# Delta-rule attention with a mixture of experts: the attention in float32 on small tiles of the array

## The chip, the cores and the metric

One core of one Trainium2 chip. The time is microseconds on the device for one execution of the whole program, the median of the runs. TensorE is PE in the profile (its weight loads PEld), VectorE is DVE, ScalarE ACT, GpSimd POOL, SyncE SP.

## The reference

Four batches, 8 heads, 768 tokens, head dimension 48 (D). Each head carries a D x D state through the tokens; the output of the heads, 384 wide, goes to a mixture of 8 experts in which a token may keep the expert of the token before it.

```python
k_n = k / (np.linalg.norm(k, axis=-1, keepdims=True) + 1e-06)
for t in range(S):
    y[:, :, t] = np.einsum('bhd,bhde->bhe', q[:, :, t], state)
    v_old = np.einsum('bhde,bhd->bhe', state, kt)
    state = state + bt[:, :, :, None] * np.einsum('bhd,bhe->bhde', kt, vt - v_old)
...
logits = np.einsum('bsd,de->bse', x, w_gate)
local_gate = 1.0 / (1.0 + np.exp(-np.einsum('bsd,de->bse', x, w_local).squeeze(-1)))
# the expert e: a fresh argmax where local_gate < 0.5 and at s == 0, else the one before
h = np.maximum(x[b, s] @ w1[e], 0.0)
out[b, s] = p[e] * (h @ w2[e])          # w1 384 x 1024, w2 1024 x 384, p the softmax of the logits
```

## The kernel before, in words

The tokens go in 24 steps of 32. In a step the 128 partitions hold 4 batches x 32 tokens, and the 8 heads lie along the free axis. Four steps make a macro step, whose preparation is shared. Every matmul operand of the attention is split into an f16 hi part and an f16 lo part, and a product is three f16 matmuls (hi hi, hi lo, lo hi).

- `K`, `norm`, `K2`, `K3` load the keys of a macro step, square and sum them (ACT, DVE), scale them by their norms, split them (`k16`), copy them apart into `KJ` (keys of two batches at columns 0 and 64), transpose `KJ` to `KT` by a DMA, and form the Gram matrices of the keys (L201).
- `T_` inverts the triangular matrices (I + beta G) of a macro step: DVE transposes (L224), a forward substitution of 15 dependent pairs of instructions on the two 16 x 16 diagonal blocks (L231, L232, nearly all on POOL), and transposes back.
- `Q` loads q and v (`qv`), splits q, spreads it to `QT`, and multiplies with the keys (L266; masked at L277).
- `Tc` adds the lower left block of the inverse by two rounds of matmuls (L292, L306), and spreads the blocks to the block-diagonal `bd`.
- `online` is the recurrence, for each half of the heads: keys times state (L329), queries times state (L336), R = v - K S (L341), U (L350), its hi and lo (L352, L353), the state in PSUM (L362, two 64-row tiles of the array), the state's hi and lo (L366, L367), the output (L372), its hi and lo (L375, L376). Every second step writes y to `xs` in DRAM, transposes it by a DMA and takes the logits (L385).

The mixture is the class `Moe`. `graph` routes the tokens of the first 20 steps, then of the last four, computes expert 0 in two lots and the expert of place 1, and loads the weights for them, all as entries of the same list as the attention. `rest` runs the other six experts (places 2 to 7) in plain program order: `upm` (L502) and `downm` (L509) on PE, `uphi` (L503) on ACT, `upt` (L504) on DVE, gathers (L490) and scatters (L492) by indirect DMAs of POOL. `overflow` is a loop that runs no iteration for tokens that fit.

The instructions of the attention and of `graph` are added to a list and issued in the order of `ORDER`, a list of numbers in the file, in which a letter names the engine where several can do the work. Buffers come from pools (`Pool_`) and are placed when their first instruction is issued. Each engine takes its own instructions in that order.

Of the kernel before, what the change touches and what calls it, by code (L numbers as in the profile page):

```python
"""Delta-rule attention followed by a top-1 mixture of experts with carried routing."""
# [13 lines left out]
class Buf:  # L15
    """a buffer of a pool, placed when its first instruction is issued"""
    def __init__(s,pool): s.pool=pool; s.slot=None; s.left=0
# [3 lines left out]
class Pool_:  # L21
    def __init__(s,tiles,name=''): s.name=name; s.tiles=tiles; s.init=[[] for _ in tiles]; s.busy=[False]*len(tiles); s.age=[-1]*len(tiles)
    def __call__(s): return Buf(s)

class Op:
    def __init__(s,fn,bufs): s.fn=fn; s.bufs=bufs; s.done=False

class Sched:
    """the instructions in program order, with what each reads, writes, writes a part of, and holds; issued in the order of ORDER.
    A function with a parameter gets the engine that ORDER names."""  # L30
    def __init__(s): s.ops=[]
    def add(s,fn,r=(),w=(),p=(),claim=()):
        bufs=list({id(x):x for x in [*r,*w,*p,*claim] if isinstance(x,Buf)}.values())
        for b in bufs: b.left+=1
        s.ops.append(Op(fn,bufs)); return s.ops[-1]
    def issue(s,order,engines):
        assert len(order)==len(s.ops)
        for n,k in enumerate(order):
            o=s.ops[int(k.rstrip("SAVPG"))]; o.done=True
            for b in o.bufs:  # L40
                p=b.pool
                if b.slot is None:
                    b.slot=min((i for i in range(len(p.tiles)) if not p.busy[i] and all(x.done for x in p.init[i])),key=lambda i:p.age[i]); p.busy[b.slot]=True
                b.left-=1
                if b.left==0: p.busy[b.slot]=False; p.age[b.slot]=n
            if k[-1] in engines: o.fn(engines[k[-1]])
            else: o.fn()


class Attn:  # L50
    NKT=9; NKJ=9; NQC=2; NBD=2; GATE=1; NKF=4; NK16=2; NQV=3; NY=2; NCMP=3; NAM=1; NLX=2; NTT=1; NTX=1; NXC=1; NPO=2; NPK=1; NPT=3; AMG=()
    def __init__(s, ctx, tc, qv,k,beta,xs,wg,wl,lg):
        s.tc=tc; s.nc=nc=tc.nc; s.xs=xs
        s.qv_,s.k,s.beta=qv,k,beta
        s.NSTEP=k.shape[0]; s.NM=s.NSTEP//4
        s.wg,s.wl,s.lg=wg,wl,lg; s.sqrts=[]
# [26 lines left out]
        s.pt=Pool_([s.pp.tile([128,512],F32,name=f"pt{i}") for i in range(s.NPT)],"pt")  # L83
        if s.GATE:
            s.wc=T([128,3,9],F32,"wc"); s.wc16=T([128,2,3,9],F16,"wc16")
            s.xt=P(1,[128,12,128],F16,"xt")
    @staticmethod
    def blk(t,z,u,p): return t[:,p,z,u,:]
    def build(s,extra=(),post=None):
        nc=s.nc; S=s.sc=Sched(); NS,NM=s.NSTEP,s.NM; add=S.add  # L90
        E_={"V":nc.vector,"G":nc.gpsimd,"A":nc.scalar,"S":nc.sync}
        s.E_=E_
# [18 lines left out]
        for f in extra: add(f)
        def zero(pool):
            for i,t in sorted(enumerate(pool.tiles),key=lambda e:(pool is s.KJ and e[0]<len(pool.tiles)-1)):
                fl=t.rearrange({3:"p a b -> p (a b)",4:"p a b c -> p (a b c)",5:"p a b c d -> p (a b c d)"}[len(t.shape)]).bitcast(F32)
                def fa(e,fl=fl):
                    if e is nc.scalar: nc.scalar.mul(fl,s.zsrc.to_broadcast(list(fl.shape)),0.0)
                    else: e.memset(fl,0.0)
                pool.init[i].append(add(fa))
# [58 lines left out]
        def K3(i,k16,k6,ii):  # L177
# [8 lines left out]
            if c==0: M["gt"]=s.gt()  # L186
# [848 lines left out]
```

## Time and profile before

| | |
|---|---|
| runs, us | 611.4, 612.09, 616.03 (median 612.09) |
| profiled execution, first to last instruction | 614.3 us |
| mean granted TensorE clock | 0.864 |
| busy PE / DVE / ACT / POOL | 473.4 / 520.8 / 346.8 / 340.8 us |
| DMA | 88.23 MB, mean 144 GB/s |
| first and last y (L376) | 76.2 and 366.6 us |

Of the profiled execution no time is known but its span, 614.3 us; it stands 2.2 us over the median of the runs. A row of a group has its line, engine, operation, what it writes and reads, partitions x elements, count, then busy us and mean ns of one, then the idle time of the engine before them and what ended it. A row of one line has min/median/max ns, and where its first and last instruction start. A row of the timeline has start, length, engine, line and count of instructions merged into one stretch. Matmuls are pipelined and their ends are modelled: how close they follow each other is read from the stretch of a burst, not from the mean of one.

### The profile page before, as it was taken

The page shows a single profiled execution, that of the slowest core. Times are in us where ns is not written, and L with a number is a line of the kernel's source. Part 1 is how long each engine was busy: PE and PEld are TensorE (multiplying, and loading weights), DVE is VectorE, ACT ScalarE, POOL GpSimd, SP SyncE. Part 2 cuts the span into 40 slices and gives each one's busy share as a digit, 9 for nine tenths or more (in the row PEclk, how much of TensorE's full clock was granted, in tenths as well). Part 3 has the DMA queues.
Part 4 walks back from the last instruction along what each step waited for, and adds up shares of the span by engine and source line. Part 5 has one row for each costly group of instructions (what it writes and reads, how often), then busy time and mean ns, then how long its engine had stood idle before and what let it go on. Part 6 is the DMA issues. An engine that isn't in the chain of part 4 may idle for free. (4 is left out here: it accounts for less than half of the span.)

```text
span 614.3 us, 19858 instructions
## 1 busy us (share of the span) xinstructions
PE 473.4 (77%) x8023; PEld 366.8 (60%) x8023; DVE 520.8 (85%) x1163; ACT 346.8 (56%) x745; POOL 340.8 (55%) x474
## 2 busy tenths in 40 slices
PE   0131677677789668687878769799999999999993
PEld 0131676677678667686777766654656555666661
DVE  7999998999899899989989998699785868597650
ACT  7567697678778777777878743213160605154220
POOL 7837686657667675757556764378843232414201
PEclk9998587588867777869867578799999999999997
DMA  5777777589899997797775617272567465666600
GB/s 191 129 163 119 165 99 131 93 162 169 126 164 165 131 145 127 122 161 158 121 191 118 127 40 253 70 227 89 145 209 211 127 194 170 187 162 221 120 16 29
DMA packets 244703, 88.23 MB, mean 144 GB/s; under 512 B 221651, under 2 KB 236047, under 8 KB 244608
## 3 DMA queue, kind: packets, MB, share of 16 engines
q1 hardware_dynamic: 241056, 76.87, 61.0%
q0 software_dynamic: 3552, 10.06, 5.2%
q8 instruction: 64, 1.05, 0.8%
q14 instruction: 31, 0.25, 0.2%
HBM read 46.34 MB, written 10.05 MB: 92 GB/s over the span
## 5 line engine op out<-in xcount | busy, mean ns | idle before, releaser
L502 PE MATMUL pt<-bd,KT 128*128 128x384 f16 (+4 forms) x432 | 92.0, 346 | 2.6 <-DVE tx L768 1.1
L502 PEld LDWEIGHTS <-KT 128*128 128x128 f16 x576 | 57.7, 102 | 44.3 <-issue 6.4
L201 PE MATMUL pt<-QC,KT 128*128 128x64 f16 x576 | 29.1, 222 | 41.7 <-DVE QC L126 28.8
L509 PE MATMUL po<-KJ,QT 128*128 128x384 f16 (+2 forms) x336 | 55.5, 326 | 0.0
L201 PEld LDWEIGHTS <-KT 128*128 128x128 f16 x576 | 26.9, 117 | 42.5 <-issue 39.6
L503 ACT ACTIVATE QT<-pt 128x384 f16<-128x384 f32 (+2 forms) x32 | 16.7, 526 | 61.9 <-PE pt L502 42.7
L509 PE MATMUL po<-KJ,L 128*128 128x384 f16 (+2 forms) x208 | 50.7, 326 | 0.0
L503 ACT ACTIVATE L<-pt 128x256 f16<-128x256 f32 (+4 forms) x40 | 18.2, 463 | 55.8 <-PE pt L502 46.1
L509 PEld LDWEIGHTS <-QT 128*128 128x128 f16 (+2 forms) x336 | 33.9, 101 | 21.1 <-issue 0.3
L329 PEld LDWEIGHTS <-KT 128*128 128x128 f16 x552 | 35.5, 117 | 16.6 <-issue 7.9
L504 DVE TENSOR_SCALAR qv<-pt 128x384 f32<-128x384 f32 (+4 forms) x56 | 33.4, 599 | 11.2 <-ACT L L503 5.5
L336 PEld LDWEIGHTS <-QT 128*128 128x128 f16 x1104 | 41.4, 107 | 1.0 <-issue 0.8
L350 PE MATMUL po<-Rs,bd 128*128 128x48 f16 x576 | 27.4, 195 | 17.7 <-DMA bd<-cmp 7.0
L492 POOL DMA_INDIRECT out_dram<-y,so x9 | 11.2, 1245 | 50.8 <-DVE y L510 50.5
L266 PE MATMUL pt<-QC,KT 128*128 128x64 f16 x576 | 31.4, 223 | 8.2 <-DVE QC L251 3.1
L329 PE MATMUL pk<-Sh,KT 128*128 128x96 f16 x368 | 30.1, 241 | 7.9 <-DVE R L341 6.5
L341 DVE SCALAR_TENSOR_TENSOR R<-pk,qv 64x192 f32<-64x192 f32 x92 | 32.4, 352 | 3.4 <-PE pk L329 1.9
L232 POOL TENSOR_TENSOR X<-X,ft 128x30 f32<-128x30 f32 (+7 forms) x75 | 31.5, 420 | 5.9
L350 PEld LDWEIGHTS <-bd 128*128 128x128 f16 x576 | 22.2, 104 | 20.2 <-issue 12.0
L509 PE MATMUL po<-KJ,X 128*128 128x384 f16 (+2 forms) x104 | 33.9, 326 | 0.0
L362 PE MATMUL Sps<-Us,KJ 64*128 64x48 f16 x1104 | 29.2, 195 | 5.4 <-DVE Us L353 4.1
L292 PE MATMUL pt<-XC,bd 128*128 128x16 f16 x576 | 21.0, 191 | 15.7 <-DVE XC L126 6.5
(316 smaller groups left out, 1503.4 us busy)
## 6 DMA issues: line engine op xcount, KB each, us to landing
KT<-in_moe_w_dram SPq DMA_DIRECT2D x24, 512.0 KB, 4.5
qv<-in_qv_dram SPq DMA_DIRECT2D x24, 448.0 KB, 4.7
KT<-in_moe_w_dram SPq DMA_DIRECT2D x20, 384.0 KB, 3.3
xs<-y SPq DMA_DIRECT2D x12, 384.0 KB, 4.4
KJ<-in_moe_w_dram SPq DMA_DIRECT2D x12, 384.0 KB, 4.6
kf<-in_k_dram SPq DMA_DIRECT2D x10, 384.0 KB, 4.2
bd<-cmp SPq DMA_DIRECT2D x58, 64.0 KB, 3.7
KJ<-k SPq DMA_DIRECT2D x65, 48.0 KB, 3.6
```

Of the source, the lines that this page charges most:

```text
L201: nc.tensor.matmul(gv[:,u,:],KT.t[:,z,u,:],KC.t[:,y,u].rearrange("r p t -> r (p t)"),start=(x==0),stop=(x==2),skip_group_check=True)
L232: eng.tensor_tensor(x[:,:,j+1:,0:k],x[:,:,j+1:,0:k],tv,op=ALU.subtract)
L266: nc.tensor.matmul(gv[:,u,:],KT.t[:,z,u,:],QC.t[:,y,u].rearrange("r p t -> r (p t)"),start=(x==0),stop=(x==2),skip_group_check=True)
L329: for uu in range(4): nc.tensor.matmul(pkv()[:,uu],KT.t[:,z,4*g+uu,:],S_.t[:,:,uu,:],start=(y_==0 and z==0 and uu==0),stop=(y_==1),skip_gr ...
L336: for p in range(2): nc.tensor.matmul(psv()[:,1,uu,:],s.blk(QT.t,z,4*g+uu,p),S_.t[:,p,uu,:],start=(y_==0 and z==0 and uu==0 and p==0),stop ...
L341: add(lambda R=R,pkv=pkv,us=us,q=q,p=p:nc.vector.scalar_tensor_tensor(R.t[q],pkv()[q,:,p,:],-2.0**-10,vb()[q,us,:],op0=ALU.mult,op1=ALU.ad ...
L350: for uu in range(4): nc.tensor.matmul(psv()[:,0,uu,:],bdv()[:,a_,4*g+uu,:],Rs.t[:,b,uu,:],start=(i==0 and b==0 and a_==2 and uu==0),stop= ...
L362: nc.tensor.matmul(s.Sps[:,p,48*u:48*u+48],KJ.t[q,a_,u,:],Us.t[q,b,uu,:],start=(i==0 and u==0 and b==0 and a_==0),stop=False,skip_group_ch ...
L502: for k in range(3): s.nc.tensor.matmul(ps,s.wv(W[k],k)[:,a,0,128*f:128*f+128],xT[:,3*b+k,:],start=(x==0 and k==0),stop=(x==2 and k==2))
L503: def uphi(s,h,ps): s.nc.scalar.activation(h,ps,AF.Relu,scale=2.0**-6)
L504: def upt(s,t,ps): s.nc.vector.tensor_scalar(t,ps,0.0,2.0**-6,op0=ALU.max,op1=ALU.mult)
L509: s.nc.tensor.matmul(po[0:m],h(a,f)[:,c:c+m],s.wv(W[k],k)[:,b,f%2,:],start=(x==0 and f==0),stop=(x==2 and f==7))
```

## The change

The attention (the class `Attn`) and the scheduler are written anew; of `Moe`, the arithmetic and the order in `rest` stay.

- The host lays k and q side by side by column (`kq`: step, pair of batches, the 48 dimensions as rows, then head, batch pair, k or q, token) beside k and v by token (`kv`). The key transposes by DMA, `KJ`, `KT`, `QT`, `QC`, `k16` and `bd` are gone.
- Matmuls are float32 calls on tiles of the array: 64 x 32 for the products over the 48 dimensions, 32 x 32 for those over 16 or 32 tokens, 32 x 64 for the state. Each batch has a tile of its own, so a product of a head is four calls.
- Nothing is split into hi and lo but y, for the mixture. The norms are read from the diagonal of the Gram matrix, and fold into beta and v.
- `ORDER` is gone. Each entry names its engines and a cost, and a list scheduler in the kernel (`Sched.order`) sorts them when the program is built: of the entries that could start within 120 ns of the earliest one, the one with the longest way to the end goes first, on the engine where it would end first.
- Pools: one `W` of 24 tiles for the keys and queries of a step and for expert weights; `po` 1 (before 2), `pk` 2 (before 1), `pt` 3 as before. The substitution is on DVE for the first macro step and on POOL after it. A macro step is prepared while the one before it runs. The weights of expert 0 are added behind step 8.

```diff
 class Sched:
-    """the instructions in program order, with what each reads, writes, writes a part of, and holds; issued in the order of ORDER.
-    A function with a parameter gets the engine that ORDER names."""
-    def __init__(s): s.ops=[]
+    HOP=70; DMA=2000; BW=170.; LOOK=120
...
+            t0=min(c[0] for c in cand)
+            t,o,x=max((c for c in cand if c[0]<=t0+s.LOOK),key=lambda c:(c[1].pri-(c[1].c[c[2]]-min(c[1].c.values()))*0-c[0]*.0,-c[0]-c[1].c[c[2]]))
...
 class Attn:
-    NKT=9; NKJ=9; NQC=2; NBD=2; GATE=1; NKF=4; NK16=2; NQV=3; NY=2; NCMP=3; NAM=1; NLX=2; NTT=1; NTX=1; NXC=1; NPO=2; NPK=1; NPT=3; AMG=()
+    NKV=5; NAM=8; NW=24; NLX=1; NPO=1; NPK=2; NPT=3; NKF=4; NFT=3; NS_=4; GATE=1
...
+        H=[(h,h%2,h//2,slice(32*h,32*h+32),slice(64*(h%2),64*(h%2)+48)) for h in range(4)]
...
+        def K(i):
+            m,c=divmod(i,4); M=mac[m]; D=st[i]
+            KQ=D["KQ"]=s.W(); g=s.pt(); am=D["am"]=s.am()
+            for j in range(2): add(lambda j=j:nc.sync.dma_start(KQ.t[64*j:64*j+48].rearrange("r u p z t -> r (u p z t)"),s.kq_[i,j]),p=[KQ],e='S',c=196608)
...
+                for u in range(8):
+                    for h,j,p,q,d in H: MM(g.t[q,64*u:64*u+64],KQ.t[d,u,p,0,:],KQ.t[d,u,p].rearrange("r z t -> r (z t)"),start=(u==0),stop=True,skip_group_check=True,tile_position=(64*j,32*h))
+            add(f,r=[KQ],w=[g],claim=[gt,am],e='P',c=900)
+            add(lambda:nc.scalar.copy(gt.t.rearrange("p t (u c) -> p u t c",c=4)[:,:,:,c],gv()[:,:,0,:]),r=[g],p=[gt],e='A',c=ca(256))
+            add(lambda:nc.vector.tensor_tensor(am.t,gv()[:,:,1,:],s.mask.unsqueeze(1).to_broadcast([128,8,32]),op=ALU.mult),r=[g,"mask"],w=[am],c=cv(256)+50)
...
+        def Tc(i):
...
+                        o=slice(32*h,32*h+16); MM(g.t[q,16*u:16*u+16],gt.t[o,:,4*u+c],TX.t[o,:,4*u+c],start=(u==0),stop=True,skip_group_check=True,tile_position=(32*h,32*h))
+            add(f1,r=[gt,TX],w=[g],claim=[QQ],e='P',c=620)
+            add(lambda:nc.scalar.copy(QQ.t[:,:,0:16],g.t[:,0:128].rearrange("p (u c) -> p u c",u=8)),r=[g],w=[QQ],e='A',c=ca(128))
...
+                    for h,j,p,q,d in H: MM(g.t[q,128+16*u:144+16*u],QQ.t[q,u,:],TT.t[q,16:32,4*u+c],start=False,stop=True,skip_group_check=True,tile_position=(32*h,32*h))
...
+            add(lambda:nc.vector.tensor_tensor(vv(),vv(),g.t[:,128:256].rearrange("p (u t) -> p u t",u=8),op=ALU.subtract),r=[g,TT],w=[(TT,c)],c=cv(128)+50)
+            add(lambda:nc.sync.dma_start(kv.t.rearrange("p z c -> p (z c)"),s.kv_[i]),w=[kv],e='S',c=393216)
...
+        def online(i):
+            py=s.po(); yv=lambda a,b:py.t[:,48*a:48*b].rearrange("p (u e) -> p u e",e=48)
...
+                            for h,j,p,q,d in H: MM(pk.t[q,48*uu:48*uu+48],KQ.t[d,4*g+uu,p,0,:],Sb.t[d,p,uu,:],start=(uu==0),stop=True,skip_group_check=True,tile_position=(64*j,32*h))
...
+                    add(lambda R=R,pk=pk,vg=vg:nc.vector.tensor_tensor(R.t.rearrange("p u e -> p (u e)"),vg(),pk.t[:,0:192],op=ALU.subtract),r=[pk,(kv,1)],w=[R],claim=[kv],c=cv(192)+40)
...
+                        for h,j,p,q,d in H: MM(pk.t[q,192+48*uu:240+48*uu],TT.t[q,:,4*(4*g+uu)+c],Rv()[q,uu,:],start=(i==0 and uu==0),stop=True,skip_group_check=True,tile_position=(32*h,32*h))
+                add(p1,r=[(TT,c),Rk],w=[pk],claim=[TT,kv],e='P',c=360)
+                add(lambda Us=Us,pk=pk:nc.scalar.copy(Us.t.rearrange("p u e -> p (u e)"),pk.t[:,192:384]),r=[pk],w=[Us],e='A',c=ca(192))
...
+                            for h,j,p,q,d in H: MM(s.Sps[d,p,48*u:48*u+48],kv.t[q,0,48*u:48*u+48],Us.t[q,uu,:],start=(i==0 and u==0),stop=False,skip_group_check=True,tile_position=(32*h,64*j))
...
+                    add(lambda Sn=Sn,g=g:nc.scalar.copy(Sn.t[0:112].rearrange("p h u e -> p h (u e)"),s.Sps[0:112,:,192*g:192*g+192]),r=["Sps"],w=[Sn],e='A',c=ca(384))
...
+        for m in range(-1,NM):
+            if m+1<NM:
+                for i in range(4*m+4,4*m+8): K(i)
+                T_(m+1)
+            if m>=0:
+                for i in range(4*m,4*m+4):
+                    Tc(i); online(i)
+                    if i in pre: pre[i](S,s)
```

More of the change, by code (lines that the diff above doesn't have):

```diff
@@ L15, with __init__ @@
 class Buf:
-    def __init__(s,pool): s.pool=pool; s.slot=None; s.left=0
+    def __init__(s,pool): s.pool=pool; s.slot=None; s.ops=[]; s.left=0; s.no=len(pool.bufs); pool.bufs.append(s)
     @property
@@ L21, with __init__, idle, at @@
 class Pool_:
-    def __init__(s,tiles,name=''): s.name=name; s.tiles=tiles; s.init=[[] for _ in tiles]; s.busy=[False]*len(tiles); s.age=[-1]*len(tiles)
+    def __init__(s,tiles,name='',free=False): s.free=free; s.name=name; s.tiles=tiles; s.bufs=[]; s.init=[[] for _ in tiles]; s.user=[None]*len(tiles); s.next=0
     def __call__(s): return Buf(s)
+    def idle(s): return [i for i,u in enumerate(s.user) if (u is None or u.left==0) and all(q.end is not None for q in s.init[i])]
+    def at(s,i): return max([0.]+[q.end for q in s.init[i]]+[q.end for q in (s.user[i].ops if s.user[i] else ())])
@@ L33, in add @@
         bufs=list({id(x):x for x in [*r,*w,*p,*claim] if isinstance(x,Buf)}.values())
[L34 to L39, printed above, removed]
+        o=Op(fn,bufs,e,c); o.boost=pri; k=lambda x:id(x) if isinstance(x,Buf) else (id(x[0]),)+x[1:] if isinstance(x,tuple) and isinstance(x[0],Buf) else x
+        for b in bufs: b.ops.append(o); b.left+=1
@@ L40, in issue @@
             for b in o.bufs:
-                p=b.pool
                 if b.slot is None:
[L43 to L46, printed above, removed]
+                    p=b.pool
+                    b.slot=min(p.idle(),key=p.at)
+                    p.user[b.slot]=b; p.next+=1
@@ new lines, in order @@
+            for b in o.bufs: b.left-=1
+            y='G' if x=='I' else x
+            busy=60. if x=='S' else 1150. if x=='I' else o.c[x]
+            E[y]=t+busy
+            if x in 'SI':
+                dma=max(dma,t)+o.c[x]/s.BW; o.end=dma+(s.DMA if x=='S' else 2500)
+            else: o.end=t+busy+(190 if x=='P' else s.HOP)
+            out.append((o,x)); s.when.append((t,busy,x,o)); avail.remove(o)
+            for q in o.succ:
+                q.need-=1; q.ready=max(q.ready,o.end)
+                if not q.need: avail.append(q)
@@ L47, in issue @@
+        assert len(out)==len(s.ops)
+        s.end=max(o.end for o in s.ops)
+        return out
+    def issue(s,engines):
+        for o,x in s.order():
+            if o.takes: o.fn(engines[x])
             else: o.fn()
 class Attn:
-    NKT=9; NKJ=9; NQC=2; NBD=2; GATE=1; NKF=4; NK16=2; NQV=3; NY=2; NCMP=3; NAM=1; NLX=2; NTT=1; NTX=1; NXC=1; NPO=2; NPK=1; NPT=3; AMG=()
-    def __init__(s, ctx, tc, qv,k,beta,xs,wg,wl,lg):
+    NKV=5; NAM=8; NW=24; NLX=1; NPO=1; NPK=2; NPT=3; NKF=4; NFT=3; NS_=4; GATE=1
@@ L82, in __init__ @@
         s.pk=Pool_([s.pp.tile([128,512],F32,name=f"pk{i}") for i in range(s.NPK)],"pk")
[L83 to L92, printed above, removed]
+        s.pt=Pool_([s.pp.tile([128,512],F32,name=f"pt{i}") for i in range(s.NPT)],"pt",True)
@@ L111, in build @@
[L111 to L118, printed above, removed]
@@ L995 @@
     with tc.manual_schedule():
[L996 to L997 removed]
+        A=Attn(ctx,tc,kq,kv,beta,xs,wg,wl,lg,M.CAP)
+        A.build(M.consts(),{8:M.early},M.graph).issue(A.E_)
         M.rest(A)
```

705 lines of the change are left out of this document (243 added, 462 removed).

## The prediction

> **What bounds the kernel now.** I read the page's first two parts, then the table of stages, then single lines for where each stage ends.
>
> ```profile
> span 614.3 us, 19858 instructions
> PE 473.4 (77%) x8023; PEld 366.8 (60%) x8023; DVE 520.8 (85%) x1163; ACT 346.8 (56%) x745; POOL 340.8 (55%) x474
> PEclk9998587588867777869867578799999999999997
> ```
> ```profile
> 60.00:75.00 15.00, 8.44 (x216) 7.97 (x216) 14.73 (x35) 8.68 (x23) 10.70 (x10) 0.50 0.75 165
> ...
> 150.00:200.00 50.00, 40.34 (x1087) 37.88 (x1086) 46.28 (x117) 39.92 (x98) 32.53 (x57) 0.76 0.94 159
> ...
> 250.00:300.00 50.00, 39.26 (x1147) 36.88 (x1149) 45.81 (x121) 38.64 (x94) 34.49 (x65) 0.83 0.83 145
> ...
> 470.00:520.00 50.00, 50.00 (x310) 29.19 (x309) 38.56 (x71) 19.38 (x29) 15.47 (x13) 1.00 0.56 163
> ```
> ```profile
> L376 DVE SCALAR_TENSOR_TENSOR y<-po,y x48: 303/347/359, 76.2 to 366.6; 128x192 f16<-128x192 f32 x48
> ```
>
> The columns of a stage are its length, then busy time (and instructions) of PE, weight loads, DVE, ACT and POOL, the granted TensorE clock, the DMA engines' share and GB/s. In 85% busy DVE two kernels are averaged. From 150 to 300 us DVE is busy 46 of 50 us and PE 40, at a clock of 0.76 to 0.83: the attention is bound by VectorE, with PE and the DMA engines (0.83 to 0.94) close behind. From 470 us PE is busy 50 of 50 at clock 1.00: the mixture is bound by PE. L376 writes a step's y: first at 76.2 us, last at 366.6. So the time is a sum of three: **76.2 us to the first y, 23 steps of (366.6 - 76.2)/23 = 12.6 us, and 614.3 - 366.6 = 247.7 us behind the last y**. The change rewrites what makes the first two.
>
> **The third term.** The experts (`rest`, `upm`, `downm`) keep their instructions. Routing and expert 0 (`graph`) keep theirs too; the order comes from the new scheduler, and 24 tiles of pool `W` stand where 18 of `KT` and `KJ` stood. Four steps, which will be shorter, cover the routing of the first 20 steps, so some of expert 0 may slide behind the last y; against that, less DVE work is left over. I take 250 us, between 243 and 262.
>
> **What goes.** The f16 hi and lo parts of k, q, X, T, R, U and S, the block-diagonal copies (`bd`, `QT`, `KJ`), the DMA transposes of the keys, the squares and norms from a second load of k. What stays of DVE, ACT and POOL work I price by rows of the same shape:
>
> ```profile
> L341 DVE SCALAR_TENSOR_TENSOR R<-pk,qv 64x192 f32<-64x192 f32 x92 | 32.4, 352 | 3.4 <-PE pk L329 1.9
> L232 POOL TENSOR_TENSOR X<-X,ft 128x30 f32<-128x30 f32 (+7 forms) x75 | 31.5, 420 | 5.9
> L231 POOL TENSOR_TENSOR ft<-L,X 128x30 f32<-128x30 f32 (+7 forms) x75 | 29.6, 395 | 5.4
> L367 DVE SCALAR_TENSOR_TENSOR Sl<-Sps,Sh 128x384 f16<-128x384 f32 x46 | 25.0, 543 | 1.2 <-ACT Sh L366 0.8
> L366 ACT ACTIVATE Sh<-Sps 128x384 f16<-128x384 f32 x46 | 22.3, 485 | 4.8 <-PE Sps L362 4.6
> L277 DVE TENSOR_TENSOR am<-pt,mask 64x256 f32<-64x256 f32 x48 | 20.1, 420 | 0.9
> L207 ACT COPY gt<-pt 64x256 f32<-64x256 f32 x47 | 17.0, 364 | 6.1 <-PE pt L201 5.4
> L352 ACT ACTIVATE Us<-po 128x192 f16<-128x192 f32 x48 | 15.7, 328 | 20.1 <-PE po L350 19.6
> L224 DVE STREAM_TRANSPOSE L<-gt 128x256 f32<-128x256 f32 x24 | 14.7, 619 | 0.3 <-ACT gt L207 0.2
> L308 DVE SCALAR_TENSOR_TENSOR TT<-pt,mneg,TT 128x128 f32<-128x128 f32 x24 | 10.3, 428 | 0.4 <-PE pt L306 0.3
> L241 DVE STREAM_TRANSPOSE TT<-X 128x256 f32<-128x256 f32 x24 | 10.0, 426 | 0.1
> L232 DVE TENSOR_TENSOR X<-X,ft 128x30 f32<-128x30 f32 (+7 forms) x15 | 6.1, 405 | 0.5
> L231 DVE TENSOR_TENSOR ft<-L,X 128x30 f32<-128x30 f32 (+7 forms) x15 | 5.6, 376 | 0.4
> L164 DVE RECIPROCAL rr<-t 128x32 f32<-128x32 f32 x5 | 1.7, 344 | 0.0
> ```
>
> DVE in a step: am 0.42 (both halves in one now), two R at 0.35, the subtraction from TT 0.43, y's lo 0.54, v by the norms 0.55 (a 384-element pass, like y's). Once in four steps: ten transposes at 0.43 to 0.62, ten small ones at no more than 0.34, two products of 256 at some 0.5 (L277's kind): 9 us, so 2.2 a step. Sum **4.9 us**. ACT: 0.36 for gt, 0.3 for QQ (less than L352's 0.33), two U at 0.33, two S and y at 0.49: **2.8 us**. POOL: 15 x (0.395 + 0.420) us of substitution in four steps, and a clear of X: **3.3 us**. None of them carries 12.6 us any more.
>
> **The DMA engines.** By the shapes, a step brings 393 KB of kq and 393 KB of k and v, writes 197 KB of xs and transposes 197 KB: 1.18 MB. At 145 to 159 GB/s, the rate of the old attention, that is 7.4 to 8.1 us; at the 163/0.56 = 291 GB/s that the large rows of the weights would reach at full share, 4.1 us. The key loads have rows of 4 KB, so I take it nearer the lower end, 5 us, hidden behind PE. Expert 0's weights (3.1 MB) come on top in some steps.
>
> **PE, which I expect to bound.** A step has 256 calls now: 32 in `K` (64 columns moving), 32 in each half of `Tc` (16 columns), and ten groups of 16 (48 columns: KS, qS, U, the state, y, twice). Before it had 264 in f16, so the count doesn't fall. The price of a call is what no row shows.
>
> ```profile
> 200.02 0.27 PE L362 MATMUL Sps<-Us,KJ 64*128 64x48 f16 x8 [0.47 <-DVE Us L353]
> 200.23 0.47 PE L350 MATMUL po<-Rs,bd 128*128 128x48 f16 x12
> ...
> 200.95 0.50 PE L329 MATMUL pk<-Sh,KT 128*128 128x96 f16 x8
> ...
> 202.44 0.37 PE L362 MATMUL Sps<-Us,KJ 64*128 64x48 f16 x16
> ```
> ```profile
> 376.07 0.30 PEld L576 LDWEIGHTS pt<-sc,blk 128*128 128x128 f32 x2 [0.96 <-issue]
> ```
> ```profile
> 371.95 0.60 PE L385 MATMUL pt<-wc,xt 128*128 128x9 f16 x18
> ```
> ```profile
> L362 PE MATMUL Sps<-Us,KJ x1104: 178/192/221, 73.5 to 350.9; 64*128 64x48 f16 x184
> ```
> ```profile
> L329 PE MATMUL pk<-Sh,KT 128*128 128x96 f16 x368 | 30.1, 241 | 7.9 <-DVE R L341 6.5 <-DVE QT L126 1.0 <-ACT Sh L366 0.2
> ```
> ```profile
> L576 PEld LDWEIGHTS pt<-sc,blk x4: 186/238/334, 325.7 to 376.2; 128*128 128x128 f32 x4
> L576 PE MATMUL pt<-sc,blk x4: 244/317/400, 325.7 to 376.2; 128*128 128x20 f32 x2, 128*128 128x4 f32 x2
> ```
>
> Four readings. (1) Two calls of L576 stand as four loads and four matmuls: a float32 call is a pair of each. (2) Two f32 loads of 128 columns take 0.30 us where one takes 0.19, so they start 0.11 us apart: 0.85 ns a column. The f16 stream of L329 starts (0.50 - 0.24)/7 = 0.037 us apart for 96 columns: 0.39 ns a column. I take 0.82 ns a column for f32, in load and stream. (3) L362 puts two 64-row tiles side by side: 16 matmuls of 48 columns start (0.37 - 0.19)/15 = 12 ns apart, so two tiles turn over every 24 ns, where the full array of L350 needs 24 ns for one. Tiles do overlap. (4) L362's eight end at 200.29, so the last starts at 200.10, and L350 at another tile size starts 0.13 us later instead of 0.024: a change of tile size costs 0.1 us.
>
> If the four tiles of a round run at once, 48 columns cost 2 x 40 ns a round, a group of four rounds 0.32 us; `K` has eight rounds of 2 x 52 ns, 0.83 us; `Tc` twice eight rounds of 2 x 26 ns (the load of 32 columns), 0.83. Sum 0.83 + 0.83 + 3.2 = 4.9 us, and half of L385's 0.60: 5.2 at full clock. At the granted clock of the stages above, some 0.78, 6.6 us. Program order changes the tile size about 12 times a step: 1.2 us. With 0.3 us of waits, **8.1 us a step**. Bounds: 6.4 at full clock without waits; one tile at a time 21 (below). Matmuls 12 ns apart, as close as L362 ever shows, would make 512 x 12 = 6.1 in place of 4.9, so 9.6. A half's chain of a step is KS, R, U, its copy, the state, its copy: three groups at 0.32 + 0.19 us, 0.35 + 0.33 + 0.49, together 2.7 us; two halves in a row 5.4, under 8.1, so the chain is hidden while PE has other work. The new waits: `po` has one buffer, so the next step's qS waits for both passes over y, 0.49 + 0.54, beside four groups of KS and state; and what the fixed order puts behind a waiting group on PE waits with it. The 0.3 us stand for these, between nothing and the 2.7 of a half's chain laid bare.
>
> **The first term.**
>
> ```profile
> 0.81 1.84 SPq L139 DMA_DIRECT2D kf<-in_k_dram  x4
> ```
> ```profile
> 3.38 1.00 ACT L144 ACTIVATE QC<-kf 128x384 f32<-128x384 f32 x2
> ```
>
> A load issued at 0.81 us is used at 3.38; eight kq loads at 0.46 us each put four steps' keys on chip by about 8 us. Then `K` 1.2 with the last step's, gt 0.4, four transposes 2.5, norms 2.5, products 1.1, the first substitution on DVE 15 x (0.376 + 0.405) = 11.7, six transposes 3.0, `Tc` 2.2, U and y 2.5. First y at **36 us** for 76.2, between 30 and 45.
>
> **Sum.** 36 + 23 x 8.1 + 250 = 472 us beside the profiled 614.3. That execution's span stands 2.2 us over the median of the runs, 612.09, so **470 us**. The range of this case alone, steps of 7 to 10.3 us: 445 to 521.
>
> **Rivals.** Break-even is a step of (614.3 - 36 - 250)/23 = 14.3 us.
>
> *The tiles wait for each other, the slower side.* 160 calls of 80 ns, 32 of 104, 64 of 52 one after another are 19.5 us, with changes and logits 21: 36 + 483 + 250 - 2 = 767 us. For it: no row shows more than two tiles at once, nor f32 in one. Against it: L362's two do overlap. Chance 0.08.
>
> *Only the calls that write one bank from four row tiles wait* (`Tc`, U and y; KS, qS, `K` and the state pair rows with other columns or banks). Then 3.3 for `Tc`, 64 x 80 ns = 5.1 for U and y, 0.83 + 6 x 0.32 for the rest: 11.2, with changes and logits 12.7 a step: 576 us. L362's two tiles write two banks, so it neither shows nor excludes this. The Trainium skill, page "TensorEngine Tiling (Array Packing)", section Restrictions and Gotchas, states just that: different row tiles cannot access the same PSUM bank at once. No run here shows it. Chance 0.12.
>
> *The clock stays at half*, as in 60 to 75 us (0.50 with PE busy 8.4 of 15), since short bursts of a quarter of the array may not lift it: 5.2/0.5 + 1.2 = 11.6 a step, 551 us. Against it: 0.76 and more as soon as PE is busy 80%. Chance 0.13.
>
> *Each matmul has a floor of one turn-over*, 24 ns as L350's, tiles or not: 512 x 24 ns = 12.3, with changes and logits 13.8: 601 us, nearly no change. L362's 12 ns speaks against it. The Trainium skill, "TensorE: Matmul & The Clock Gate", Part 1, gives a floor of about 25 ns start to start however few columns; the trace agrees for one tile and not for two. Chance 0.04.
>
> *All goes well*: full clock, no waits, 6.4 a step, 431 us. Chance 0.14.
>
> **How the numbers follow.** Main case 0.49. 428 to 590 leaves out the waiting tiles (0.08), the floor (0.04) and a third of the best case: 0.17. Faster by over 1% (about what a measurement of this kernel tells from no change): main, best, half clock, bank and most of the floor: 0.89; within 1%: 0.02; slower: 0.09.
>
> **What would show it.** The first y's instruction near 36 us and the last near 222; DVE below 65% and PE above 85% busy in the attention; state matmuls of 16 calls (32 records) in 0.5 us with their drain; 247 to 253 us behind the last y. The prediction is wrong if PE's rounds take over 150 ns, if the clock lies under 0.6, or if the scheduler's order leaves PE waiting for DVE copies, which shows as idle PE before KS.

## The result, and the profile after

The changed kernel takes **696.21 us** (median of four runs, 691.12 to 697.3) against 612.28 for the kernel before on the same chip (611.4 to 616.03): an estimated ratio of 1.1336, 95% interval 1.1281 to 1.1391. The forecast was 470. Of all profiles below, one is of a slow run, that of `e4_bf16_once` (539.37 us, its other run 528.79). The profiled execution has a span of 694.0 us. The page of the changed kernel:

```profile
span 694.0 us, 30098 instructions
PE 534.0 (77%) x13903; PEld 406.0 (58%) x13903; DVE 300.0 (43%) x719; ACT 158.9 (23%) x308; POOL 142.8 (21%) x278
PEclk9999998565555555555555558686899999999997
q8 instruction: 109, 1.79, 1.1%
```

VectorE, which bounded the attention before, is down from 521 busy us to 300, as forecast, and PE's 8023 matmul records have become 13903 (a float32 call is two). The last row is a queue that I had read past: 109 packets and 1.79 MB, so 16 KB each. Its packets go with PE's instructions: 13903 matmuls and as many loads are 27806 = 108.6 x 256, and in the kernel before 16046 = 62.7 x 256 stand beside 64 packets.

The line that writes a step's y, which cuts the time into its three terms, and two stretches of the table of stages:

```profile
L284 DVE SCALAR_TENSOR_TENSOR y<-po,y x24: 524/554/569, 67.7 to 400.1; 128x384 f16<-128x384 f32 x24
```
```profile
100.00:150.00 50.00, 41.47 (x1718) 36.04 (x1714) 16.33 (x41) 12.82 (x29) 13.10 (x31) 0.74 0.31 87
150.00:200.00 50.00, 39.52 (x1710) 35.19 (x1705) 16.15 (x43) 11.10 (x27) 13.65 (x32) 0.50 0.24 60
```

| | first y | a step | behind the last y |
|---|---|---|---|
| before | 76.2 | 12.6 | 247.7 |
| forecast | 36 | 8.1 | 250 |
| after | 67.7 | (400.1 - 67.7)/23 = 14.45 | 694.0 - 400.1 = 293.9 |

All three terms missed: 31.7 us, 23 x 6.35 = 146 us and 43.9 us make the 222 between 472 and 694. In the two stretches shown no engine but PE is busy even 17 of 50 us, the DMA engines are at 0.24 to 0.31, and PE is busy only 40 of 50. So what holds a step? The waits of PE between 100 and 350 us, with the sum in us, the number of them and the longest:

```profile
PE pt L236 <- issue: 13.9, 10, 5.1
PE pt L231 <- issue: 10.3, 9, 2.5
PE po L260 <- issue: 7.4, 6, 2.0
PE po L281 <- issue: 6.5, 5, 4.3
PE Sps L273 <- issue: 5.4, 5, 3.1
PE pk L254 <- issue: 3.6, 6, 1.2
PE pt L236 <- DVE nT L206: 3.3, 1, 3.3
PE pt L185 <- issue: 2.5, 3, 1.7
...
PE pk L266 <- issue: 0.9, 3, 0.5
```

"issue" is a wait for nothing that the profile shows. It is 50.5 of the 250 us, 2.9 us a step; waits for another engine are small. The order in time on PE shows where it falls:

```profile
203.75 0.54 PE L260 MATMUL po<-S,W 48*32 48x48 f32 x14
206.27 0.55 PE L260 MATMUL po<-S,W 48*32 48x48 f32 x17 [1.98 <-issue]
206.61 0.29 PE L254 MATMUL pk<-S,W 48*32 48x48 f32 x3
206.63 0.28 PE L260 MATMUL po<-S,W 48*32 48x48 f32 x1
206.69 0.86 PE L254 MATMUL pk<-S,W 48*32 48x48 f32 x29
207.47 1.50 PE L281 MATMUL po<-Us,am 32*32 32x48 f32 x64
208.91 0.56 PE L273 MATMUL Sps<-Us,kv 32*48 32x48 f32 x14
210.28 0.64 PE L273 MATMUL Sps<-Us,kv 32*48 32x48 f32 x18 [0.81 <-issue]
```

PE stops in the middle of a group, 14 records in, where no buffer can be missing. Between the stops lie 17 + 3 + 1 + 29 + 64 + 14 = 128 matmuls and as many loads: **256 instructions**, of 64 bytes each if they fill one 16 KB packet of the instruction queue. In this trace such packets start 3.3 us apart at the closest and 3.7 at the median of the attention. A step has 1024 instructions for its calls and 18 for the logits, 4.07 blocks. Between the first and the last y it issues only 945 of them, 3.69 blocks, because products `K` of later steps run ahead (2874 PE instructions start before the first y): 3.69 blocks of 3.92 us are the 14.45. That gave theory F: **the supply of instructions to PE, a block of 256 per 3.3 to 3.9 us, sets the step**. The rivals: A, the array's own time at the half clock of 150 to 200 us; D, waits for copies.

The start times in the trace tie the stops to the packets. Between 100 and 350 us PE has 59 stops of more than 0.3 us from one start to the next. Of these, 52 end 1.2 to 1.6 us after a packet of that queue has landed (median 1.39), and 51 of the 52 lie whole multiples of 256 instructions apart, but for one instruction now and then. After such a stop the next packet never starts sooner than 1.03 us after PE has gone on (median 1.14), and it takes 1.0 us. So, as these stops show it, the fetch of a block starts only when PE has begun the one before, and some 1.1 + 1.0 + 1.4 = 3.5 us pass from block to block, however little work the block holds.

### The profile page after: what moved, and what is told of

It reads as the page before. It is cut to its first block, busy times and chain, and to the rows that moved or that the text cites. A ratio compares the mean times of both kernels' runs of the same rounds, so it can differ in the third digit from the quotient of the medians.

```text
span 694.0 us, 30098 instructions
## 1 busy us (share of the span) xinstructions
PE 534.0 (77%) x13903; PEld 406.0 (58%) x13903; DVE 300.0 (43%) x719; ACT 158.9 (23%) x308; POOL 142.8 (21%) x278
## 3 DMA queue, kind: packets, MB, share of 16 engines
q8 instruction: 109, 1.79, 1.1%
## 5 line engine op out<-in xcount | busy, mean ns | idle before, releaser
L408 PE MATMUL pt<-xT,W 128*128 128x384 f16 (+4 forms) x432 | 90.0, 352 | 13.2 <-DMA xT<-kv 13.2
L415 PEld LDWEIGHTS <-W 128*128 128x128 f16 (+4 forms) x696 | 70.2, 101 | 46.0 <-issue 4.1
L408 PEld LDWEIGHTS <-W 128*128 128x128 f16 x576 | 59.1, 103 | 58.8 <-DMA xT<-kv 13.3
L257 DVE TENSOR_TENSOR R<-kv,pk 128x192 f32<-128x192 f32 x46 | 16.2, 353 | 108.6 <-PE pk L254 108.6
L185 PE MATMUL pt<-W 48*32 48x64 f32 x1536 | 48.5, 307 | 19.0 <-issue 14.1
L393 DVE SCALAR_TENSOR_TENSOR W<-W,W 128x768 f16<-128x768 f32 (+1 forms) x50 | 53.1, 1069 | 3.5 <-ACT W L391 3.4
L415 PE MATMUL po<-W,W 128*128 128x384 f16 (+3 forms) x294 | 50.4, 326 | 3.0 <-DVE kf L416 3.0
L254 PE MATMUL pk<-S,W 48*32 48x48 f32 x1472 | 44.4, 276 | 10.0 <-issue 7.5
L231 PE MATMUL pt<-TX,gt 16*32 16x16 f32 x1536 | 30.0, 214 | 27.6 <-issue 19.1
L281 PE MATMUL po<-Us,am 32*32 32x48 f32 x1536 | 42.6, 273 | 10.1 <-issue 9.9
L391 ACT ACTIVATE W<-W 128x768 f16<-128x768 f32 (+1 forms) x50 | 45.3, 929 | 17.1 <-DMA W<-in_moe_w_dram 17.0
L415 PE MATMUL pk<-W,W 128*128 128x384 f16 (+2 forms) x288 | 48.5, 326 | 0.0
L273 PE MATMUL Sps<-Us,kv 32*48 32x48 f32 x1472 | 42.3, 276 | 5.4 <-issue 5.4
L260 PE MATMUL po<-S,W 48*32 48x48 f32 x1472 | 38.8, 278 | 9.4 <-issue 7.7
L231 PEld LDWEIGHTS pt<-TX,gt 16*32 16x32 f32 x1536 | 27.2, 149 | 30.1 <-issue 29.3
L254 PEld LDWEIGHTS pk<-S,W 48*32 48x32 f32 x1472 | 34.1, 157 | 16.5 <-issue 10.1
L281 PEld LDWEIGHTS po<-Us,am 32*32 32x32 f32 x1536 | 33.9, 156 | 15.2 <-issue 12.2
```

Of the source, the lines that this page charges most:

```text
L185: for h,j,p,q,d in H: MM(g.t[q,64*u:64*u+64],KQ.t[d,u,p,0,:],KQ.t[d,u,p].rearrange("r z t -> r (z t)"),start=(u==0),stop=True,skip_group_c ...
L231: o=slice(32*h,32*h+16); MM(g.t[q,16*u:16*u+16],gt.t[o,:,4*u+c],TX.t[o,:,4*u+c],start=(u==0),stop=True,skip_group_check=True,tile_position ...
L254: for h,j,p,q,d in H: MM(pk.t[q,48*uu:48*uu+48],KQ.t[d,4*g+uu,p,0,:],Sb.t[d,p,uu,:],start=(uu==0),stop=True,skip_group_check=True,tile_pos ...
L260: for h,j,p,q,d in H: MM(py.t[q,192*g+48*uu:192*g+48*uu+48],KQ.t[d,4*g+uu,p,1,:],Sb.t[d,p,uu,:],start=(g==0 and uu==0),stop=False,skip_gro ...
L273: for h,j,p,q,d in H: MM(s.Sps[d,p,48*u:48*u+48],kv.t[q,0,48*u:48*u+48],Us.t[q,uu,:],start=(i==0 and u==0),stop=False,skip_group_check=Tru ...
L281: for h,j,p,q,d in H: MM(py.t[q,192*g+48*uu:192*g+48*uu+48],am.t[q,4*g+uu,:],Us.t[q,uu,:],start=(i==0 and g==0 and uu==0),stop=True,skip_g ...
```

## The experiments

Times are medians (of e4_bf16_once the shorter of its two runs); first y, step and the stretch behind the last y are read from the y line of each profile, as above.

| run | us | first y | step | behind |
|---|---|---|---|---|
| e1_array | 696.65 | 65.7 | 14.55 | 296.5 |
| e2_instr | 782.35 | 82.9 | 17.35 | 293.4 |
| e3_bf16_twice | 687.22 | 63.4 | 14.17 | 293.7 |
| e4_bf16_once | 528.79 | 48.8 | 8.36 | 296.5 |
| e5_planner | 693.25 | 86.0 | 13.75 | 288.5 |
| e6_subst | 659.98 | 67.5 | 13.56 | 280.2 |
| e7_lead | 702.27 | 68.5 | 14.92 | 294.6 |
| e8_all | 625.64 | 71.7 | 11.38 | 290.4 |
| e9_pool | 669.65 | 68.6 | 14.43 | 267.0 |
| e10_best | 603.21 | 66.4 | 11.79 | 265.6 |
| e11_hold | 720.13 | 71.1 | 15.38 | 293.6 |
| e12_best_hold | 606.7 | 70.6 | 11.70 | 264.9 |
| e13_before_256 | 653.06 | 79.6 | 14.13 | 246.7 |
| e14_before_512 | 732.89 | 86.3 | 17.14 | 247.1 |

### What sets the step

**Array time without instructions** (e1_array):

```diff
 def f():
+    for _ in range(2): MM(g.t[:,0:512],s.dz[:,0:128],s.dz,start=True,stop=True,...)
     for u in range(8):
```
(the same two ahead of Tc's first products)

> Four matmuls of the whole array over 512 columns of f16 zeros are added to each step (two ahead of the products of K, two ahead of the first products of Tc): at half clock 4 x 0.43 = 1.7 us more of array time, but only 8 instructions more. Theory A (the step is PE's array time at half clock: 512 matmuls x 18.7 ns = 9.6 us, twelve changes of tile size x 0.28 = 3.4, logits 0.8, together 13.8 of the 14.45): the step grows by 1.7 to 16.1 us, the whole by some 39 us to 735; or, if the added full-array work lifts the clock, the step falls. Theory F (the step is the supply of instructions, about 1042 a step in blocks of 256 at 3.5 us a block): the idle time before a block shrinks, the step stays at 14.3 to 14.8, the whole at 693 to 705. Theory D (PE waits for copies by other engines): the step stays too, and no idle time falls on every 256th instruction.

The step went from 14.45 to 14.55, though PE was busy 208 of the 250 us from 100 to 350, in place of 192. 0.8 to 1.7 us of array work a step vanished in the idle time. A falls.

**Instructions without array time** (e2_instr), in each half of Tc:

```diff
 for h,j,p,q,d in H: MM(g.t[q,16*u:16*u+16],...)
+for _ in range(2):
+    for h,j,p,q,d in H: MM(g.t[q,300:302],s.dz[q,0:32],s.dz[q,0:2],start=False,...,tile_position=(32*h,32*h))
```

> 128 matmuls of two f16 columns on 32x32 tiles are added to each step, onto columns that nothing reads: 256 instructions (one block more), with 32 rounds of four tiles of some 25 to 45 ns at half clock, 0.8 to 1.5 us of array time. Theory A: the step grows by 0.8 to 1.5 us, the whole by 20 to 35 us, to 715 to 730. Theory F: one block more, 3.5 us a step, the whole by 80 us to 776.

17.35 a step, and 86 us more in all for 24 blocks, so 3.6 us each. As F has it; the step grew by 2.9 and not 3.5, since more instructions ran ahead of the first y (3936 in place of 2874).

**The same count of shorter calls, and half of it** (e3_bf16_twice, e4_bf16_once):

```diff
-MM(pk.t[...],KQ.t[d,4*g+uu,p,0,:],Sb.t[d,p,uu,:],...)
+MM(pk.t[...],hb(KQ.t)[d,4*g+uu,p,0,:],hb(Sb.t)[d,p,uu,:],...)   # hb: the upper half of each word, bfloat16
+MM(pk.t[...],hb(KQ.t)[d,4*g+uu,p,0,:],s.zb[d,0:48],start=False,...)   # e3 alone
```

> The attention's matmuls read the upper 16 bits of each operand as bfloat16, and each call is issued a second time with a moving tile of zeros: the same number of calls' instructions as before the cut (a float32 call stands as two loads and two matmuls, a bfloat16 call as one of each), each of them shorter. y, and with it the routing, is computed from cut operands. Theory A: 128 rounds of four tiles at 40 ns (48 columns of 0.39 ns at half clock) = 5.1 us, changes 3.4, logits 0.8: a step of 9.3 us, the whole some 575 us. Theory F: still 1042 instructions and four blocks, 14 us a step, 680 to 696 us.

> The same cut operands, each call issued once: half the instructions (512 for the calls and 18 pairs of the logits, 2.1 blocks a step). Theory F: 2.1 x 3.5 = 7.3 us a step, the whole 694 - 23 x 7.1 = 531 us. Theory A: 64 rounds at 40 ns = 2.6 us, changes 3.4, logits 0.8 = 6.8 us, or the chain of one half, 5.4 to 7; the whole 515 to 530. The two do not part here but in the run with each call twice; this one bounds what the attention costs when PE has little to do.

14.17 with each call twice. With each once it is 8.36, over the 7.3 and 6.8 of the two sides: with half the instructions PE waits for other engines too. The waits of PE in e3_bf16_twice, 100 to 350 us (L159 is the added call):

```profile
PE pt L159 <- issue: 49.6, 26, 6.6
PE po L159 <- issue: 27.1, 17, 4.0
PE pk L159 <- issue: 20.8, 13, 2.8
PE Sps L159 <- issue: 11.1, 7, 2.3
```

The shorter calls turned into idle time: 108.6 us of "issue" in place of 50.5, and the step stayed. That is the cleanest of the tests: array time halved (86 ns at the median for eight matmuls, where the float32 calls take 160), instructions equal, time within 2%. All 64 of its stops that end 1.2 to 1.7 us after a packet lie exact multiples of 256 instructions apart. Between the first and last y a block takes 3.92 us in the changed kernel, 3.91 in e1_array, 3.81 in e2_instr and 3.85 in e3_bf16_twice, whatever its work; in the kernel before it takes 6.14.

**And the clock?** It doubles the calls, but it doesn't set the step. The changed kernel has a short stretch at full clock, and then a long one at half:

```profile
137.40:144.20 6.80, 3.17 (x192) 2.63 (x180) 2.99 (x5) 2.65 (x5) 5.83 (x13) 1.00 0.48 137
144.20:200.00 55.80, 44.63 (x1898) 39.64 (x1901) 16.97 (x45) 11.81 (x28) 14.24 (x35) 0.50 0.26 66
```
```profile
139.36 1.10 PE L185 MATMUL pt<-W 48*32 48x64 f32 x64
140.28 0.52 PE L254 MATMUL pk<-S,W 48*32 48x48 f32 x32
...
144.33 0.55 PE L273 MATMUL Sps<-Us,kv 32*48 32x48 f32 x12 [3.13 <-issue]
```

At 1.00, 32 records of L254 take 0.52 us, and the eight records of a round of four calls 85 ns; at 0.50 it is 29 in 0.86 us (above) and 160 ns a round. The full clock gained nothing here: PE stopped for 3.13 us at the end of the block. And e3_bf16_twice, with the array's time halved, kept its step. In e9_pool (below; the attention is unchanged) a row seems to say otherwise:

```profile
150.00:200.00 50.00, 39.18 (x1686) 34.88 (x1683) 16.09 (x43) 10.46 (x25) 13.45 (x32) 1.00 0.24 63
```
```profile
152.52 1.50 PE L281 MATMUL po<-Us,am 32*32 32x48 f32 x64
```

The 1.00 isn't a reading: the trace of e9_pool has no record of the clock before 290.6 us (the changed kernel's has none before 113.5), and the profile shows 1.00 where there is none. The calls tell the clock. In the traces of the float32 attention, the rounds of L254, L260 and L281 take 85 ns (median) in stretches recorded at full clock and 160 in those recorded at half, and without a record, as in e9_pool at this time, 160. So the attention ran at half clock nearly all the time.

**Is it the chip, or this kernel's calls?** Two runs add cheap f16 matmuls to the kernel *before*:

```diff
 def f1():   # and f2
     ...
+    for k in range(16):   # 32 in e14
+        for h in range(4): nc.tensor.matmul(g.t[32*h:32*h+32,300:302],bdv()[32*h:32*h+32,2,0,0:32],...,tile_position=(32*h,32*h))
```

> The kernel before, with 128 matmuls of two f16 columns on 32x32 tiles added to each step behind the two products of the block inverse, onto columns that nothing reads: 528 + 256 = 784 PE instructions a step. Theory F (3.1 blocks of 3.7 us = 11.3, still under the 12.6 that VectorE sets): steps of 12.6 to 13.0, the whole at 612 to 622 (some 1 us of array time a step lies partly on the path). Rival (each instruction costs PE time whatever the number, as the 86 us of the same addition to the changed kernel would also have it): 3.5 us a step, some 690.

> The same with 256 matmuls, so 1040 instructions a step, as many as the changed kernel has. Theory F: 4.06 blocks of 3.6 to 3.9 us = 14.6 to 15.8 a step, 46 to 74 us more: 658 to 686, with idle time of PE every 256 instructions. Rival (array time only): twice the addition of the run with 128, 612 to 640.

Waits of PE, 100 to 350 us, in the kernel before, e13_before_256 and e14_before_512, the largest three for "issue" each (before has only two):

```profile
PE Sps L362 <- issue: 0.8, 2, 0.5
...
PE pt L385 <- issue: 0.4, 1, 0.4
```
```profile
PE Sps L366 <- issue: 7.8, 5, 2.3
PE po L354 <- issue: 6.6, 3, 2.9
PE pt L310 <- issue: 6.1, 7, 2.3
```
```profile
PE pt L310 <- issue: 18.8, 11, 3.3
PE po L340 <- issue: 12.2, 5, 4.1
PE pk L333 <- issue: 6.3, 3, 4.2
```

The first 256 cost 1.5 us a step, between the two sides (0 to 0.4, and 3.5). The next 256 cost 3.0 more, and e14_before_512 took longer than either side had it. So the limit is not one of float32 calls, but it is no clean threshold of the average either. 784 instructions in 12.6 us leave 4.1 us a block, more than the 3.3 to 3.7 needed; yet the added ones come in bursts (in e14 128 matmuls with their loads, a whole block, in 1.3 us). Since the fetch of a block starts only when PE has begun the one before, PE stands idle behind a burst though the average would fit. Stops of more than 0.3 us that end 1.1 to 1.75 us after a packet make some 0.5 us a step in the kernel before, 2.1 in e13 and 4.0 in e14, most of the 1.5 and 4.5 us that the step grew by. The DMA engines, at 0.57 to 0.83 here, may slow the blocks too (median 4.45 us apart in e13 with PE not always asking, 4.0 in e14), and the granted clock fell with the idle time (0.78 in the kernel before, 0.73 and 0.66, as means of the five stages from 100 to 350 us); how much each of these adds isn't settled.

### Where the other two terms went

**The planner's costs** (e5_planner):

```diff
-add(f,r=[KQ],w=[g],claim=[gt,am],e='P',c=900)
+add(f,r=[KQ],w=[g],claim=[gt,am],e='P',c=1850)   # Tc's halves 620 to 1850, groups 360 to 920
```

> Only the costs that the list scheduler assumes for PE's attention groups are changed (K 0.9 to 1.85 us, each half of Tc 0.62 to 1.85, a group of 16 calls 0.36 to 0.92: half a block, half a block and a quarter of a block of 256 instructions at 3.7 us). The scheduler had planned steps of 6.9 us and now plans 13.5; the instructions are the same, their order changes. Theory O (the 294 us behind the last y, against 247.7 before, come from an order made for steps of 6.9 us: the routing of the first 20 steps is planned beside too few of them): the stretch behind the last y falls to 250 to 262 us, steps stay at 14.3 to 14.6, the whole at 650 to 662. Rival C (the 88 us from the last y to place 1 are one chain of routing, gathers and lots that no order shortens): 290 to 296 behind the last y, the whole 685 to 697.

288.5 us behind the last y, and 693.25 for the whole: theory O is worth 5 us of the 44. The step fell to 13.75 because more instructions ran ahead (3978 before the first y, which came at 86.0 us); a block still took 3.91 us.

**The results' buffers** (e9_pool). The routing of the last four steps needs the logits and nothing else, but on VectorE it came 29 us after them, and place 1 waited:

```diff
-po=A.pt() if z==0 else A.po(); y=A.kf(); a=a0+j
+po=A.pt() if z==0 else A.po(); y=A.S_(); a=a0+j
```

> Only the buffers of the lots' results y change: they come from pool S_ (four buffers, free once the states are done) instead of kf. kf has four buffers, handed out strictly in program order: three to the routing of the first 20 steps, the fourth and the next to lot 0's two results, so the routing of the last four steps can be issued only behind lot 0's down products. In the changed kernel the logits were there at 406.5 us, the routing of the last steps began on VectorE at 435.5 and place 1 at 487.9. Theory B (this hold is what lengthens the stretch): routing of the last steps within 10 us of its logits, lot 1 and place 1 earlier, 255 to 270 us behind the last y in place of 294, the whole 660 to 672. Rival: the stretch is bound by the work in it (conversions of weights, gathers, lots): 285 to 294, the whole 685 to 697.

The order in time, first of the changed kernel, then of e9_pool: the first two operations of that routing, and the first up product of place 1.

```profile
406.66 0.19 DVE L466 TENSOR_REDUCE mxl<-lg 128x4 f32<-128x32 f32 x1
...
435.50 0.18 DVE L467 TENSOR_TENSOR kf<-lg,mxl 128x32 f32<-128x32 f32 x1
...
487.94 4.32 PE L408 MATMUL pt<-xT,W 128*128 128x496 f16 x10 [13.18 <-DMA xT<-kv]
```
```profile
407.24 0.18 DVE L466 TENSOR_REDUCE mxl<-lg 128x4 f32<-128x32 f32 x1
407.46 0.19 DVE L467 TENSOR_TENSOR kf<-lg,mxl 128x32 f32<-128x32 f32 x1
...
453.89 5.81 PE L408 MATMUL pt<-xT,W 128*128 128x496 f16 x27
```

L467 is the first operation that needs a buffer of kf. With its buffer free it follows at once, place 1 starts without a gap 34 us earlier, and 26.9 of the 43.9 us are gone. Theory B holds. What is left, 267.0 against the forecast 250, is probably lot 0 for the greater part (not tested): its first gather starts at 406.5 us here, 6 us behind the last y, and in the kernel before at 347.7, 19 us ahead of it.

**The start** (e7_lead, e11_hold). Both hold back key loads:

```diff
 add(lambda j=j:nc.sync.dma_start(KQ...,s.kq_[i,j]),p=[KQ],e='S',c=196608)
+i>=8 and S.ops[-1].pre.add(st[i-8]['kop'])   # e7: behind K of step i-8; e11: 'p1', behind U of step i-8
```

> The key loads of step i are held back until the products K of step i-8 are issued; nothing else changes. In the changed kernel the first blocks of instructions are fetched at 12.4, 20.2, 28.1 and 41.6 us, 7.8 us apart, while the DMA engines are 0.97 busy; from 45 us on, at a share of 0.2 to 0.3, they are 3.3 to 4 us apart. Theory Q (the fetch waits behind the loads on the same DMA engines): with the first loads spread out, blocks come every 4 us from the start, the first y falls from 67.7 to 50 to 58 us, the whole by 10 to 18 us to 678 to 686. Rival: the early spacing has another cause (PE waits for keys or substitution): first y 65 to 70, the whole unchanged.

> The key loads of step i (from the ninth on) wait for the U products of step i-8, so that only eight steps' keys (3.1 MB) and five loads of k and v (2.0 MB) stand at the start; the run that held them back to the products K left the DMA engines at 1.04 for 40 us all the same. Theory Q (a block's fetch waits behind the loads): blocks 7.8 us apart only until about 20 us, then 3.5 to 4; first y 55 to 62 in place of 67.7, the whole 683 to 691. Rival: the start waits for the first substitution on VectorE, which ends at 38.5, and 7 blocks behind it: first y 65 to 68, the whole 690 to 700.

e7_lead hardly held anything, since K runs ahead too. e11_hold did; the stages of the changed kernel and of e11_hold:

```profile
20.00:30.00 10.00, 3.63 (x127) 3.39 (x127) 9.03 (x41) 1.57 (x3) 0.96 (x1) 1.00 1.05 229
```
```profile
20.00:40.00 20.00, 4.91 (x162) 4.42 (x162) 18.38 (x74) 2.63 (x5) 1.86 (x2) 1.00 0.25 84
```

In e11_hold the loads are through at some 24 us (a DMA share of 1.05 from 23 to 24 us, 0.39 in the next). The third packet of instructions then started 1.65 us after PE had gone on, in place of 5.3 in the changed kernel, and 4.1 us behind the second in place of 7.9. So blocks do wait behind loads, as far as one packet shows it; but the first y stayed at 71.1 and the later steps lost (15.38). Theory Q is right on the mechanism and wrong on the time: the start is held by VectorE (18.4 of 20 us busy with the first substitution and its transposes, done at 40 us) and after it by seven blocks of PE instructions that the order puts ahead of the first y (1850 instructions from 40.6 to 67.7 us).

### A version that comes out under both

Fewer instructions without a change of precision: the inverse of a 32x32 block by plain substitution, so Tc's 64 calls go (e6_subst); the planner's costs and held keys with it (e8_all); with the results' buffers and without held keys (e10_best); with held keys (e12_best_hold).

```diff
-for j in range(15):
-    n=15-j; k=j+1; e=2*n*k; ft=s.ft()      # two 16x16 blocks, then Tc's products
+for j in range(31):
+    n=31-j; k=j+1; e=n*k; ft=s.ft()        # one 32x32 block
-def f1(): ... MM(...gt.t[o,:,4*u+c],TX.t[o,:,4*u+c]...)   # and QQ, f2, the subtraction from TT
```

> The inverse of a 32x32 block is made by 31 steps of substitution on GpSimd (VectorE for the first four steps) instead of 15 steps on two 16x16 blocks and the two products of Tc: 64 calls, so 256 of the 1042 PE instructions of a step, are gone. Theory F: 786 instructions = 3.07 blocks of 3.5 to 3.9 us, a step of 10.8 to 12.0 us in place of 14.45, the whole at 694 - 23 x 2.45 to 3.65 = 610 to 638, with the stretch behind the last y still near 294. Rival P: the longer substitution, some 36 us of GpSimd in four steps by the scheduler's cost formula, takes over as the bound, or it and VectorE slow each other: GpSimd busy over 90% and steps of 12.5 us or more, the whole over 650. First y near 65: the 16 further steps of substitution add some 6 us on VectorE, and two products less take one block away.

> The three edits together: planner costs, full substitution, key loads held back. If they add: first y 52 to 60 us, 23 steps of 10.8 to 12.0, 250 to 262 us behind the last y: 555 to 598 us, below both kernels. If the substitution on GpSimd bounds the step (12.5 us or more), 600 or more.

> Full substitution in place of Tc's products, planner costs by blocks, and the results of the lots from S_ (key loads not held back). Steps of 11.4 us as measured with the first two, first y 66 to 72, 255 to 270 behind the last y if theory B holds: 583 to 604 us, below both kernels. If it doesn't: 612 to 625.

> e10_best with the key loads held back as in e11_hold. First y 6 to 12 us earlier than in e10_best if theory Q holds, else the same within 3; steps of 11.4 us; 575 to 600 us.

e6_subst alone missed, with 13.56 a step. Step and time came out as rival P had them, but GpSimd was busy 57% of 100 to 350 us and not over 90%: in the order made for cheap PE groups, PE ran into the substitution. Its largest wait of PE, 100 to 350 us:

```profile
PE pk L250 <- DVE TT L220: 34.5, 5, 11.8
```

With costs that are near the truth (e8_all) this wait is 1.6 us and the step 11.38, 2.84 blocks of 4.00 us between the first and last y. The sum of e8_all still missed, by 12 us in the first y (31 steps of substitution on VectorE) and by 28 behind the last, before e9_pool had found the reason. e10_best, its page and its y line:

```profile
span 603.2 us, 24096 instructions
PE 472.4 (78%) x10831; PEld 350.5 (58%) x10831; DVE 306.9 (51%) x718; ACT 154.5 (26%) x286; POOL 259.3 (43%) x445
```
```profile
L268 DVE SCALAR_TENSOR_TENSOR y<-po,y x24: 542/556/559, 66.4 to 337.6; 128x384 f16<-128x384 f32 x24
```

**603.21 us against 613.03, ratio 0.9842 (0.9806 to 0.9878)**: 1.6% under the kernel before, a small gain that is clear of the noise, and 93 us under the changed one, with the attention still in float32 on small tiles. Its forecast was 583 to 604. Holding the keys (606.7, ratio 0.9877, 0.983 to 0.9924) adds nothing: its forecast, 575 to 600 with a first y no later than 69.4, missed.

## Why the prediction was wrong, point by point

- *"PE, which I expect to bound"*: right on the engine, wrong on what of it. I priced calls by the array and looked at no supply of instructions; "512 matmuls" stood in the text, and the queue that feeds them on the page. This is the step that failed, a term that the sum didn't have: 2.9 us a step of "issue", 66 us in all, and, since it is a floor, no saving on the array could have brought the step under 14.2 (e3_bf16_twice).
- *"At the granted clock of the stages above, some 0.78, 6.6 us"*: the term that was mis-sized. The clock of the old attention was carried over, and the new one ran at 0.50 nearly throughout; why it stayed there isn't shown. The rounds came out twice as long, 160 ns where 79 was forecast at full clock. With the medians of the trace for eight records (160 ns in the ten groups, 213 in `K`, 120 and 107 in `Tc`) a step's calls take 10 x 4 x 0.160 + 8 x 0.213 + 8 x 0.227 = 9.9 us, with 0.5 of logits 10.4 in place of 6.6, and with the 1.2 of tile changes 11.6. That is the 11.6 of the rival of the half clock, so this rival was right on the array's time; its 551 us missed for want of the supply. Without waits for instructions the time would have been some 694 - 66 = 628 us, by estimate. The parts don't add up to 14.45 to the tenth, since a part of `K` runs ahead. The prediction had named both "PE's rounds over 150 ns" and a clock "under 0.6" as what would make it wrong.
- *"If the four tiles of a round run at once"*: they do. In stretches recorded at full clock the rounds of L254, L260 and L281 take 85 ns, of L273 90, of `K` 112, where 79 and 104 were forecast. Only U (116) and the first product of `Tc` (120, at either clock) are well over; why is open.
- *The bank rival* (four row tiles writing one bank wait for each other): refuted. L281 writes one bank from four row tiles, L254 from two, and both show 85 ns a round at full clock. The Trainium skill, page "TensorEngine Tiling (Array Packing)", section Restrictions and Gotchas, has the rule; the trace doesn't show it.
- *The floor of a turn-over for each matmul*: also refuted; L231's records start 15 ns apart.
- *First y at 36 us*: the chain on VectorE ended at 40 and not 30, as the products `K` of the fourth step were cut short by PE's first stop (from 11.7 to 15.6 us, behind 446 instructions) and the next four steps' transposes came in between; then seven blocks, 27 us, in place of 4.7.
- *250 us behind the last y*, "between 243 and 262": 293.9. I had named the cause, "some of expert 0 may slide behind the last y", and given it 12 us. Not seen was a pool of four buffers handed out in program order, worth 26.9.
- The chances: main case, best case, half clock and bank make 0.88, so 0.89 holds a quarter of the floor's 0.04 and not most of it.
- Right: the work of VectorE, ACT and GpSimd (43%, 23% and 21% busy), no bound by the DMA engines, and that the copies' chains hide.

## What to carry to other kernels

Count PE's instructions per stage, loads and float32's second passes included, and hold 256 of them against some 3.5 us before pricing the array; cheap calls on small tiles reach that limit long before the array is full, and a burst reaches it though the average fits. If "issue" waits fall in the middle of a group and 256 instructions apart, only fewer instructions help: shorter or faster ones turn into idle time. Read the clock off the calls too: a row of 1.00 can stand for no record at all. A list scheduler is as good as its costs and its pools: a buffer pool that is handed out in program order can hold back work that needs nothing else.

## What was not expected of the hardware

- Blocks of 256 PE instructions start 3.3 us apart at best, 3.7 at the median of the attention (stages at a DMA share of 0.15 to 0.54) and 7.8 with the DMA engines at 1.05. PE goes on 1.4 us after a block has landed, and the next one's fetch starts 1.0 us later or more. The Trainium skill, page "Runtime: NRT & Kernel Launch", section Instruction fetch mechanics, has the blocks of 256 instructions, and the traces agree; that the cost of crossing one is "mostly hidden" the traces contradict: 50.5 of 250 us idle in the changed kernel, 108.6 in e3_bf16_twice.
- A round of four float32 calls of 48 columns took 85 ns where the trace has a record of full clock and 160 ns where it has one of half. The Trainium skill, page "TensorE: Matmul & The Clock Gate", Part 1, has a matmul take twice as long at half the clock, and these calls agree but for a few ns.
- Four tiles of 32 rows, and four tiles in two pairs of 64 rows, run side by side: the 85 ns are hardly more than the 79 that I had estimated for one call alone at full clock.
